# GELU through tanh, attention normalisation through a DMA transpose, and a scale folded into the last residual

## The chip, the core and the metric

The kernel runs on one core of a Trainium2 chip. The time is device microseconds for one execution, the median of several runs. The engines are TensorE (PE in the profile; PEld is its weight load), VectorE (DVE), ScalarE (ACT), GpSimd (POOL) and SyncE (SP), which issues most of the DMAs. Each engine works through its own list of instructions in order, and they meet through semaphores.

## The reference

One transformer block on 2048 tokens of width 640, in bf16: attention with 32 query heads of 20 columns over one shared key and value head, then a gated MLP of width 1536.

```python
x = A_x
h = x + _A_ref(_layernorm(x), A_wq, A_wk, A_wv, A_wo)
h2 = h + _B_ref(_layernorm(h), B_w_gate, B_w_up, B_w_down)

# _A_ref
q = (x @ wq) split into 32 heads; k = x @ wk; v = x @ wv
p = softmax(q k^T * 20 ** -0.5)
return (p v, heads side by side) @ wo

# _B_ref
g = x @ w_gate
u = x @ w_up
h = gelu(g, approximate=True) * u      # the tanh form
return h @ w_down
```

## The kernel before

The 16 token tiles of 128 rows are put into chunks: seven of two tiles, two of one (CHUNKS). A chunk's heads are cut into units, 32 in all; a unit is 512 query columns in four row groups. For each unit there are 16 packs, one for each tile of keys. A pack is four score matmuls (line 1083) that fill four PSUM banks of 512 columns, so that there are 512 packs and 2048 score tiles in all.

A score tile is made into exp in one of two ways. ScalarE takes one or two banks in one instruction (line 1423, tile pa). Or VectorE takes one bank (line 1509, tile pd): it computes an integer whose bits, read as bf16, are a rough exponential. Two shifted copies of that integer are added to it for accuracy, by POOL for both at once (line 1486), by POOL for one (line 1472), or by VectorE (line 1466). The product with the values (line 1162) runs over pa and over the three parts of pd. It collects a unit's sums and its row sums in one PSUM bank. Banks 0 to 5 are for scores; banks 6 and 7 are shared by those sums and by all other matmul jobs.

When a unit is done, its sums are copied to SBUF (osb, line 1189; two slots), transposed by four matmuls with the identity into a PSUM bank (on_job), and there divided by the row sums: a reciprocal (line 674, rcp) and one or two products (line 668) that write onq. When a chunk's units are all done, a DMA transposes onq into onT (line 699), the output projection follows and its result is added to xh (line 728). The second normalisation writes xn_tmp (line 472), and another DMA transpose on SP (line 464) makes xn2T.

The MLP of a chunk (a batch) runs while the next chunks' attention is under way. Its 12 gate blocks are worked in jobs of 512 columns, six for a batch of two tiles, three for a batch of one. A gate job's PSUM bank is copied to gbuf by VectorE (line 809). After the last gate job of the batch, ScalarE runs the GELU over gbuf in place, 1536 columns at a time (line 829), with a load of the function table in front and another one in front of the next exp. Each up job then multiplies gbuf by its bank (line 846), the down job adds its result to xh (line 864), and an output DMA stores it (line 862). For gate jobs that finish after the last exp, ScalarE takes the GELU straight from PSUM (line 811).

The order of every engine's list is made when the kernel is built, by a planner that plays the engines forward with a price for each instruction: c_act, c_dve, POOL_ADD and POOL_ADD2, in ns. Waiting work stands as jobs (matmul pieces for a bank) and tasks (one instruction), each with a priority; a task is placed when the plan says that its inputs are there. For each pack, issue_qk decides how many of its four tiles VectorE gets:

```python
burst = A > 3000.0                     # work queued on ScalarE, with the GELUs and their loads
...
elif burst:
    n = 4 if Dv < 2500.0 else 2
elif Dv > TH0:                         # work queued on VectorE; TH0 is 1500
    n = 0
elif Dv < TH2 or (SP2 and Dv < SP2D and len(pend[1]) + len(pend[2]) < 2 * SP2P
                  and stall(t, 1, fb) + 1382.0 - stall(t, 2, fb) - 956.0 > SP2G):
    n = 2
else:
    n = 1
```

Here pend holds shifted copies that nobody has made yet. VectorE makes them itself only when PADD_LEN of them wait. The functions that the change touches, and what calls them:

Of the kernel before, what the change touches and what calls it, by code (L numbers as in the profile page):

```python
# [3 lines left out]
ACT = mybir.ActivationFunctionType  # L4
# [190 lines left out]
def bass_sequential_preLN__grouped_kv_mqa__glu_gated_geglu__prompt_kernel(  # L195
# [36 lines left out]
    PE_TO = (15,)  # L232
    NA = 16
# [3 lines left out]
    NON = 8  # L237

# [10 lines left out]
    xn2T = sb("xn2T", [P, NC_D, 1024], BF16)  # L249
# [13 lines left out]
    osb = sb("osb", [P, 2, 512], BF16)  # L263
    rcp = sb("rcp", [P, 2, 16], F32)
    onq = sb("onq", [P, NON, D], BF16)
    onT = sb("onT", [P, 4, NC_D, P], BF16)
    gbuf = sb("gbuf", [P, NFC, 512], BF16)
    ident = sb("ident", [P, P], BF16)
# [32 lines left out]
    def c_mm(n):  # L301
        return n
# [12 lines left out]
    POOL_ADD = 635.0  # L315
    POOL_ADD2 = 1200.0
# [3 lines left out]
    SP2G = 300.0  # L320
# [4 lines left out]
    PADD_LEN = 2  # L325
# [7 lines left out]
    NP0 = 4  # L333
    WQA = 1
# [44 lines left out]
    slots = {"xt": list(range(NXT)), "q": list(range(NQ)), "onT": list(range(4)), "osb": [0, 1], "rcp": [0, 1]}  # L379
# [26 lines left out]
    def ln_group(ln, tiles, prio, done):  # L406
# [27 lines left out]
        def norm(t):  # L434
# [9 lines left out]
            def then(op):  # L444
# [12 lines left out]
                def free():  # L457
                    return ln == 0 or batch_of[t] < 2 or up_left[batch_of[t] - 2] == 0
# [35 lines left out]
    for b, tl in enumerate(BATCHES):  # L494
        for i, t in enumerate(tl):
            xcol[t] = (b % 2) * 512 + i * P
# [129 lines left out]
    def on_job(u, so):  # L626
        tl, gs = u["tiles"], u["groups"]
        nt, G = len(tl), len(gs)
        pieces = []
        for j in range(4):  # L630
            pieces.append((mm((lambda j: lambda b: ps[:, b * 512 + j * P:b * 512 + (j + 1) * P])(j),
                              osb[:, so, j * P:(j + 1) * P], ident[:], True, True), c_mm(128),
                           [("osb", so), "ident"]))

        def then(b):
            slots["osb"].append(so)
            sr = slots["rcp"].pop(0)
            v5 = bank(b).rearrange("p (j r e) -> p j r e", j=4, r=4)

            def c1(op):  # L640
                cnt = [0]
                parts = []
                rv = rcp[:, sr, :].rearrange("p (j r) -> p j r", j=4)
                if nt == 4:
                    g = gs[0]
                    o = onq[:, onslot[tl[0]]:onslot[tl[0]] + 4, 4 * Dh * g:4 * Dh * (g + 1)].rearrange(
                        "p j (r d) -> p j r d", r=4)
                    parts.append((o, slice(0, 4)))
                elif nt == 2:
                    for gi, g in enumerate(gs):  # L650
                        o = onq[:, onslot[tl[0]]:onslot[tl[0]] + 2, 4 * Dh * g:4 * Dh * (g + 1)].rearrange(
                            "p j (r d) -> p j r d", r=4)
                        parts.append((o, slice(2 * gi, 2 * gi + 2)))
                else:
                    o = onq[:, onslot[tl[0]], 4 * Dh * gs[0]:4 * Dh * (gs[-1] + 1)].rearrange(
                        "p (j r d) -> p j r d", j=4, r=4)
                    parts.append((o, slice(0, 4)))

                def c2(op):
                    cnt[0] += 1  # L660
                    if cnt[0] == len(parts):
                        free_bank(b)
                        slots["rcp"].append(sr)
                        unit_normed(u)

                for o, js in parts:
                    nj = js.stop - js.start
                    dve((lambda o, js, nj: lambda e: e.tensor_tensor(  # L668
                        o, v5[:, js, :, 0:Dh], rv[:, js, :].unsqueeze(3).to_broadcast([P, nj, 4, Dh]), ALU.mult))(
                            o, js, nj), c_dve(80 * nj), [("b", b), ("rcp", sr)],  # L670
                        [("onq", onslot[t], g) for t in tl for g in (gs if nj == 4 else [gs[js.start // 2]])],
                        0.9, c2)

            dve(lambda e: e.reciprocal(rcp[:, sr, :].rearrange("p (j r) -> p j r", j=4), v5[:, :, :, Dh]), 200,
                [("b", b)], [("rcp", sr)], 0.8, c1)

        def gate():
            return bool(slots["rcp"]) and all(x in on_sent for t in tl for x in on_before[t])
        jobs.append(_Job(("on", u["id"]), 1.5, pieces, then, gate))
# [56 lines left out]
    gate_left = [NFC] * len(BATCHES)  # L736
    up_left = [NFC] * len(BATCHES)
    copied = [[] for _ in BATCHES]
# [48 lines left out]

    def gate_job(b, fc):
        n = len(BATCHES[b]) * P
        k = per_job(b)  # L790
        ks = [x for i in range(k) for x in gkeys(b, fc + i)]

        def then(bk):
            def fin(op):
                free_bank(bk)
                gate_left[b] -= k
                copied[b].append(fc)
                if gate_left[b] == 0:
                    gelu(b)

            def fin2(op):
                free_bank(bk)
                gate_left[b] -= k
                up_job(b, fc)
                if gate_left[b] == 0 and copied[b]:
                    gelu(b)
            o, i = gview(b, fc, k), bview(bk, b, k)
            if state["exps_left"] > 0:
                dve(lambda e: e.tensor_copy(o, i), c_dve(n * k), [("b", bk)], ks, 1.0, fin)
            else:  # L810
                task(("act",), lambda e: e.activation(o, i, ACT.Gelu_apprx_tanh), ("gelu", c_act(n * k)), L_ACT,
                     [("b", bk)], ks, 1.0, fin2)
        jobs.append(_Job(("gate", b, fc), 5.0, gu_pieces(wg_sb, b, fc), then, lambda: g_free(b)))

    def gelu(b):
        k = per_job(b)
        fcs = sorted(copied[b])
        runs = []
        n = len(BATCHES[b]) * P
        most = max(k, 1536 // n)  # L820
        for fc in fcs:
            if runs and runs[-1][1] == fc and fc + k - runs[-1][0] <= most:
                runs[-1][1] = fc + k
            else:
                runs.append([fc, fc + k])
        for f0, f1 in runs:
            v = gview(b, f0, f1 - f0)
            ks = [x for fc in range(f0, f1) for x in gkeys(b, fc)]
            task(("act",), (lambda v: lambda e: e.activation(v, v, ACT.Gelu_apprx_tanh))(v),
                 ("gelu", c_act(n * (f1 - f0))), L_ACT, ks, ks, 1.0,  # L830
                 (lambda f0, f1: lambda op: [up_job(b, fc) for fc in range(f0, f1, k)])(f0, f1))

    def up_job(b, fc):
        n = len(BATCHES[b]) * P
        k = per_job(b)
        ks = [x for i in range(k) for x in gkeys(b, fc + i)]

        def then(bk):
            def fin(op):
                free_bank(bk)  # L840
# [4 lines left out]
            o, i = gview(b, fc, k), bview(bk, b, k)  # L845
            dve(lambda e: e.tensor_tensor(o, i, o, ALU.mult), c_dve(n * k), [("b", bk)] + ks, ks, 1.0, fin)  # L846
# [875 lines left out]
```

The softmax here doesn't subtract the row's maximum and nothing guards it: scores larger than these inputs give would overflow.

## Time and profile before

| | |
|---|---|
| median of 9 runs | 805.67 us (803.52 to 806.87) |
| the profiled execution | 803.7 us, its span 801.8 us |
| mean granted TensorE clock | 0.979 |
| ACT busy | 749.8 us (94%) |
| PE busy | 689.9 us (86%) |
| DVE busy | 627.3 us (78%) |
| POOL busy | 585.4 us (73%) |
| score tiles | 1461 on ScalarE, 587 on VectorE |

The span is the time from the first to the last instruction; the rest of the execution's time lies around it. In the groups of the profile each row has a line of the kernel, an engine, an operation, what it writes and reads, its shape and count, then its busy time, the mean duration of one instruction and the idle time of the engine just before. An instruction's duration can overlap its neighbour's on the same engine, so that count times mean is more than the busy time.

### The profile page before, as it was taken

What the parts mean: (1) busy time and instruction counts of PE and PEld (TensorE: products, weight loads), DVE (VectorE), ACT (ScalarE), POOL (GpSimd) and SP (SyncE); (2) the same over time, 40 slices, a digit from 0 to 9 for tenths busy, and PEclk for the clock granted to TensorE, in tenths of its full rate; (3) what the DMA queues carried; (4) which work ended last, traced back from release to release, by engine and by line L of the source; (5) the groups of instructions that cost most, each with busy time, mean ns of one, the idle gap of its engine ahead of it and who ended that gap; (6) DMA issues with size and microseconds to landing.
All of it is one profiled execution on the core that took longest, in us unless ns stands there. A gap on an engine that the chain in (4) does not pass through costs nothing.

```text
span 801.8 us, 29858 instructions
## 1 busy us (share of the span) xinstructions
PE 689.9 (86%) x13162; PEld 331.5 (41%) x13162; DVE 627.3 (78%) x1156; ACT 749.8 (94%) x1065; POOL 585.4 (73%) x624
## 2 busy tenths in 40 slices
PE   4687778979978998789988799888998899887998
PEld 3332223534434443344434344334444444343457
DVE  7968889777888678977788777988779767878864
ACT  5899999999989999899999999999999999999981
POOL 4587878868767677766878678877787768776760
PEclk9999999999999899999999999999999999999999
DMA  6680001000100000000000000000010000100000
GB/s 193 128 308 2 2 10 26 3 2 2 36 18 3 2 19 19 18 3 3 19 18 19 2 3 19 19 19 2 3 35 19 4 2 19 19 18 11 11 19 18
DMA packets 40288, 21.96 MB, mean 27 GB/s; under 512 B 31328, under 2 KB 38880, under 8 KB 40160
## 3 DMA queue, kind: packets, MB, share of 16 engines
q1 hardware_dynamic: 38848, 19.61, 9.5%
q8 instruction: 105, 1.72, 0.9%
q10 hardware_dynamic: 1312, 0.44, 0.2%
q14 instruction: 23, 0.19, 0.1%
HBM read 10.21 MB, written 2.62 MB: 16 GB/s over the span
## 4 chain that ended last, share of the span: by engine, by line
PE 47%; DVE 25%; ACT 24%; issue 2%; DMA 1%; POOL 1%; POOLq 0%; DVEq 0%
ACT pa L1423 24%; PE ps L510 18%; DVE pd L1509 15%; PE ps L1083 14%; PE ps L1162 13%; PE ps L506 3%; DVE pd L1466 3%; DVE xn_tmp L472 2%; DVE osb L1189 1%; DVE stats L403 1%; DVE qT L580 1%; DVE xh L728 1%; DMA onT<-onq 1%; DVE onq L668 0%; DVE ln_vb L415 0%
## 5 line engine op out<-in xcount | busy, mean ns | idle before, releaser
L1423 ACT ACTIVATE pa<-ps 128x512 bf16<-128x512 f32 (+1 forms) x1012 | 698.6, 849 | 24.1 <-PE ps L1083 19.2
L1486 POOL TENSOR_TENSOR pd<-pd,shifts 128x512 int32<-128x512 int32 x517 | 534.1, 1041 | 168.4 <-DVE pd L1509 159.7
L1509 DVE TENSOR_SCALAR pd<-ps 128x512 uint16<-128x512 f32 x587 | 395.4, 688 | 139.9 <-PE ps L1083 129.2
L1162 PE MATMUL ps<-pd,v_ext 128*32 128x512 bf16 x1761 | 273.6, 395 | 28.1 <-DVE osb L1189 21.5
L1162 PE MATMUL ps<-pa,v_ext 128*32 128x512 bf16 x1461 | 263.6, 391 | 2.7 <-ACT pa L1423 1.3
L1083 PE MATMUL ps<-qT,kT 32*128 32x512 bf16 x2048 | 205.3, 388 | 66.9 <-DVE pd L1509 41.1
L1083 PEld LDWEIGHTS ps<-qT,kT 32*128 32x128 bf16 x2048 | 58.8, 91 | 233.2 <-DVE pd L1509 163.7
L1162 PEld LDWEIGHTS ps<-pd,v_ext 128*32 128x32 bf16 x1761 | 74.5, 97 | 78.5 <-issue 33.8
L1162 PEld LDWEIGHTS ps<-pa,v_ext 128*32 128x32 bf16 x1461 | 70.3, 96 | 42.5 <-issue 29.4
L510 PE MATMUL ps<-xn2T,wg_sb 128*32 128x256 bf16 (+1 forms) x1720 | 65.2, 276 | 0.1
L510 PE MATMUL ps<-xn2T,wu_sb 128*32 128x256 bf16 x1680 | 65.2, 277 | 0.1
L510 PE MATMUL ps<-wd_sb,gbuf 128*32 128x320 bf16 x1344 | 64.3, 301 | 0.2 <-DVE onq L668 0.2
L510 PE MATMUL ps<-xn1T,wq_pad 128*32 128x256 bf16 (+1 forms) x1440 | 51.2, 267 | 0.2
L510 PEld LDWEIGHTS ps<-xn2T,wu_sb 128*32 128x32 bf16 x1680 | 43.0, 98 | 18.5 <-issue 10.1
L510 PEld LDWEIGHTS ps<-xn2T,wg_sb 128*32 128x32 bf16 x1720 | 41.7, 97 | 17.3 <-issue 11.4
L510 PEld LDWEIGHTS ps<-wd_sb,gbuf 128*32 128x32 bf16 x1344 | 33.5, 96 | 23.7 <-issue 11.8
L510 PEld LDWEIGHTS ps<-xn1T,wq_pad 128*32 128x32 bf16 x1440 | 33.9, 98 | 13.7 <-issue 8.6
L846 DVE TENSOR_TENSOR gbuf<-ps,gbuf 128x512 bf16<-128x512 f32 x48 | 32.9, 686 | 6.6 <-PE ps L506 6.4
L1466 DVE TENSOR_SCALAR pd<-pd 128x512 uint16<-128x512 uint16 (+2 forms) x66 | 37.8, 594 | 0.0
L1472 POOL TENSOR_TENSOR pd<-pd,shifts 128x256 int32<-128x256 int32 x48 | 30.2, 635 | 3.5 <-DVE pd L1509 3.0
L403 DVE BATCH_NORM_STATS2 stats<-xh 128x6 f32<-128x320 bf16 x64 | 29.9, 477 | 1.2 <-DMA xh<-in_A_x_dram 1.0
L510 PE MATMUL ps<-wo_sb,onT 128*32 128x320 bf16 x600 | 28.5, 301 | 0.9 <-DMA onT<-onq 0.6
(71 smaller groups left out, 357.6 us busy)
## 6 DMA issues: line engine op xcount, KB each, us to landing
out_dram<-xh SPq DMA_DIRECT2D x16, 160.0 KB, 1.8
xh<-in_A_x_dram SPq DMA_DIRECT2D x3, 640.0 KB, 6.8
wg_sb<-in_B_w_gate_dram SPq DMA_DIRECT2D x1, 1920.0 KB, 9.1
wu_sb<-in_B_w_up_dram SPq DMA_DIRECT2D x1, 1920.0 KB, 13.4
wd_sb<-in_B_w_down_dram SPq DMA_DIRECT2D x1, 1920.0 KB, 18.0
wo_sb<-in_A_wo_dram SPq DMA_DIRECT2D x1, 800.0 KB, 5.1
gbuf<-in_A_wq_dram ACTq DMA_DIRECT2D x1, 400.0 KB, 4.8
gbuf<-in_A_wq_dram SPq DMA_DIRECT2D x1, 400.0 KB, 7.4
```

The costliest lines, as they stand in the source:

```text
L403: dve(lambda e: e.bn_stats(stats[:, ln, t, 6 * h:6 * h + 6], xh[:, t, h * HALF:(h + 1) * HALF]), 395, [key], [("st", ln, t, h)], prio, c)
L472: tk.fn = lambda e: e.tensor_scalar(xn_tmp[:, s, :], xh[:, t, :], mv[:, ln, t, 0:1], ln_r[:, ln, t:t + 1], ALU.subtract, ALU.mult)
L506: return e.matmul(o(b), l, r, start=st, stop=sp)
L510: ins = e.matmul(o(b)[a, :], l[:, a], r, start=st, stop=sp, tile_position=(0, 32 * j))
L846: dve(lambda e: e.tensor_tensor(o, i, o, ALU.mult), c_dve(n * k), [("b", bk)] + ks, ks, 1.0, fin)
L1083: ins = e.matmul(bank(b), kT4[32 * r:32 * r + 32, kt * P:(kt + 1) * P], qT[32 * r:32 * r + 32, s, :], start=True, stop=True, tile_position ...
L1162: ins = e.matmul(ps[32 * r:32 * r + 32, ab * 512:(ab + 1) * 512], v_ext[:, it["kt"], it["w"], :], it["ap"], start=st, stop=(j in ends), ti ...
L1423: op = plan.commit("act", lambda e: e.activation(dst, src, ACT.Exp, scale=SM_SCALE), cost, L_ACT, [("b", b0 + i) for i in range(n)], [("pa ...
L1466: return e.tensor_scalar(pd[:, w, a], pd[:, 0, a], float(CH_SHIFT[w]), None, ALU.add)
L1472: return e.tensor_tensor(pd32[:, w, h], pd32[:, 0, h], shifts[:, w - 1:w].to_broadcast([P, 256 * k]), ALU.add)
L1486: return e.tensor_tensor(pd32[:, 1:3, h], pd32[:, 0, h].unsqueeze(1).to_broadcast([P, 2, 256]), shifts[:].unsqueeze(2).to_broadcast([P, 2, ...
L1509: op = plan.commit("dve", lambda e: e.tensor_scalar(pd[:, 0, s * 512:(s + 1) * 512], bank(b), CH_A, CH_B, ALU.mult, ALU.add), c_dve(512), ...
```

## The change

- **GELU.** While exps are left, the gate bank is scaled by the square root of 0.044715 on its way into gbuf. VectorE squares it into a new tile zt (six slots) and makes the cubic (z + 1) times o in one instruction. ScalarE takes tanh of that, 512 columns at a time. The up job's bank is multiplied by (tanh + 1), and the product goes once more by gbuf. The up job starts when its tanh is done, not when the batch's GELU is. Gate jobs after the last exp keep the GELU instruction.
- **Normalisation.** For units 0 to 29 a DMA transpose on SP brings osb into a new tile onr (two slots); the reciprocal and one product read it there. Units 30 and 31 keep the identity matmuls.
- **Residual.** The factor 2 times that square root stays in gbuf and is taken out where the down-projection is added to xh.
- **Sizes and prices.** xn2T has three parts of 256 columns in place of two of 512. POOL's prices, SP2G and PADD_LEN are other numbers, and ScalarE's queue counts waiting tanh tasks without a table load.

```diff
+    PE_ON = (30, 31)
+    NZ = 6
...
-    xn2T = sb("xn2T", [P, NC_D, 1024], BF16)
+    xn2T = sb("xn2T", [P, NC_D, 768], BF16)
...
+    onr = sb("onr", [P, 2, 512], BF16)
+    zt = sb("zt", [P, NZ, 512], BF16)
...
+    def c_dve2(n):
+        return n / 1.92 + 150.0
-    POOL_ADD = 635.0
-    POOL_ADD2 = 1200.0
+    POOL_ADD = 580.0
+    POOL_ADD2 = 1010.0
-    SP2G = 300.0
+    SP2G = 200.0
-    PADD_LEN = 2
+    PADD_LEN = 3
...
+    def normed(u, so, v, key, done):
...
+            tk.fn = lambda e: e.reciprocal(rcp[:, sr, :].rearrange("p (j r) -> p j r", j=4), v4[:, :, :, Dh])
...
+            dve(lambda e: e.tensor_tensor(o, i0, i1, ALU.mult), 400, [key, ("rcp", sr)],
+                [("onq", onslot[t], g) for t in tl for g in gs], 0.9, c2)
...
+    def on_job(u, so):
+        if u["id"] in PE_ON:
...
+        tk = _Task(("sp",), None, 1330, 1500, [("osb", so)], [], 0.5, None, lambda: bool(slots["onr"]))
...
+            tk.fn = lambda e: e.dma_start_transpose(onr[:, s, :].rearrange("p (j i) -> p j i", j=4), osb[:, so, :])
...
     def gate_job(b, fc):
...
+                sq = (lambda e: e.tensor_tensor(z, o, o, ALU.mult))
...
+                    dve(sq, c_dve2(w), ks, [("z", s)], 1.0, c2)
+            def c2(op):
+                dve(lambda e: e.scalar_tensor_tensor(z, z, 1.0, o, ALU.add, ALU.mult), c_dve(w), [("z", s)] + ks,
+                    [("z", s)], 1.0, c3)
+            def c3(op):
+                task(("act",), lambda e: e.activation(zt[:, s, 0:w], zt[:, s, 0:w], ACT.Tanh, scale=GC / GK),
+                     c_act(w) + 45.0, L_ACT, [("z", s)], [("z", s)], 1.0, lambda op: up_job(b, fc, s))
             if state["exps_left"] > 0:
-                dve(lambda e: e.tensor_copy(o, i), c_dve(n * k), [("b", bk)], ks, 1.0, fin)
+                dve(lambda e: e.tensor_scalar(o, i, GK, None, ALU.mult), c_dve(w), [("b", bk)], ks, 1.0, c1)
...
-    def gelu(b):
...
-            dve(lambda e: e.tensor_tensor(o, i, o, ALU.mult), c_dve(n * k), [("b", bk)] + ks, ks, 1.0, fin)
+            if s is None:
+                dve(lambda e: e.scalar_tensor_tensor(o, i, 2.0 * GK, o, ALU.mult, ALU.mult), c_dve(w),
+                    [("b", bk)] + ks, ks, 1.0, fin)
+                return
...
+                dve(lambda e: e.tensor_tensor(o, z, o, ALU.mult), c_dve2(w), [("z", s)] + ks, ks, 1.0, fin)
+            dve(lambda e: e.scalar_tensor_tensor(z, z, 1.0, i, ALU.add, ALU.mult), c_dve(w),
+                [("b", bk), ("z", s)], [("z", s)], 1.0, c1)
...
-            dve(lambda e: e.tensor_tensor(xh[:, t, h * HALF:(h + 1) * HALF], xh[:, t, h * HALF:(h + 1) * HALF],
-                                          bank(bk, HALF), ALU.add), c_dve(HALF),
+            x = xh[:, t, h * HALF:(h + 1) * HALF]
+            dve(lambda e: e.scalar_tensor_tensor(x, bank(bk, HALF), 0.5 / GK, x, ALU.mult, ALU.add), c_dve(HALF),
...
+    def act_tasks():
+        return sum(tk.cost for tk in tasks if tk.engs[0] == "act" and not isinstance(tk.cost, tuple))
...
-        if state["tab"] == "gelu" or any(tk.engs[0] == "act" for tk in tasks):
-            A += sum(tk.cost[1] for tk in tasks if tk.engs[0] == "act" and isinstance(tk.cost, tuple)) + 1300.0
+        A += act_tasks()
-        burst = A > 3000.0
+        burst = A > BURST
```

BURST is 3000.

## Prediction

> **What bounds the kernel now.** I read the page's busy times first, then the groups with their forms kept apart, then the windows of the long middle, and last the timeline around one GELU. Busy times and groups:
>
> ```profile
> PE 689.9 (86%) x13162; PEld 331.5 (41%) x13162; DVE 627.3 (78%) x1156; ACT 749.8 (94%) x1065; POOL 585.4 (73%) x624
> ...
> L1423 ACT ACTIVATE pa<-ps 128x1024 bf16<-128x1024 f32 x449 | 487.3, 1088 | 2.5 <-PE ps L1083 2.5
> L1509 DVE TENSOR_SCALAR pd<-ps 128x512 uint16<-128x512 f32 x587 | 395.4, 688 | 139.9 <-PE ps L1083 129.2
> L1423 ACT ACTIVATE pa<-ps 128x512 bf16<-128x512 f32 x563 | 357.7, 659 | 21.6 <-PE ps L1083 16.7 <-PE ps L1162 0.2
> ...
> L846 DVE TENSOR_TENSOR gbuf<-ps,gbuf 128x512 bf16<-128x512 f32 x48 | 32.9, 686 | 6.6 <-PE ps L506 6.4
> ...
> L809 DVE CAST gbuf<-ps 128x512 bf16<-128x512 f32 x42 | 28.7, 684 | 0.3 <-PE ps L510 0.2
> ...
> L1466 DVE TENSOR_SCALAR pd<-pd 128x512 uint16<-128x512 uint16 x43 | 21.3, 500 | 0.0
> ...
> L829 ACT ACTIVATE gbuf<-gbuf 128x1536 bf16<-128x1536 bf16 x14 | 20.0, 1475 | 0.1
> L668 DVE TENSOR_TENSOR onq<-ps,rcp 128x160 bf16<-128x160 f32 x56 | 16.1, 318 | 0.7
> ...
> L829 ACT ACT_TABLE_LOAD x7 | 9.0, 1283 | 0.1
> L1423 ACT ACT_TABLE_LOAD x7 | 9.0, 1283 | 0.0
> ```
>
> The 2048 softmax tiles of 512 columns are shared: ScalarE takes 2 x 449 + 563 = 1461, VectorE (DVE) 587. A tile costs ScalarE 0.478 us (the page's 698.6 us for both forms, by 1461) and DVE 0.673 (395.4 by 587). DVE's idle time (139.9) is waiting for the next scores; ScalarE has almost none. The windows say it for the middle:
>
> ```profile
> core 0: us, PE busy (x) PEld busy (x) DVE busy (x) ACT busy (x) POOL busy (x), PEclk, DMA share, GB/s
> 40.00:760.00 720.00, 627.77 (x12058) 291.33 (x12050) 573.10 (x1006) 700.54 (x994) 550.54 (x560) 0.98 0.08 21
> 120.00:160.00 40.00, 35.59 (x700) 16.94 (x698) 34.94 (x64) 39.65 (x58) 32.76 (x34) 1.00 0.07 15
> 400.00:440.00 40.00, 33.61 (x632) 14.76 (x624) 35.18 (x66) 38.54 (x58) 31.27 (x32) 1.00 0.09 19
> ```
>
> In these 720 us ScalarE is busy 97.3% and DVE 79.6%. So ScalarE's work sets the length, and each tile that DVE takes off it shortens the whole. The chain of waits gives PE 47%, DVE 25%, ACT 24%: the three hand one set of score banks round, so no bank is late for long. Around one GELU:
>
> ```profile
> 447.74 3.68 DVE L1509 TENSOR_SCALAR pd<-ps 128x512 uint16<-128x512 f32 x6
> 448.08 1.28 ACT L829 ACT_TABLE_LOAD   x1
> 449.38 2.86 ACT L829 ACTIVATE gbuf<-gbuf 128x1536 bf16<-128x1536 bf16 x2
> 452.24 1.28 ACT L1423 ACT_TABLE_LOAD   x1
> ```
>
> ScalarE leaves the exps for 5.4 us, and DVE does six tiles in a row meanwhile: the planner's burst rule buys back part of the stop.
>
> **ScalarE, step by step.** Out: seven such stops, 20.0 + 9.0 + 9.0 = 38.0 us. In: 42 tanh of 512 columns (as many as L809 has gates; the six GELUs after the last exp stay). A third of the 1475 ns GELU is 0.49 us, the 512-wide exp lasts 0.66, its share per tile is 0.478. Bounds 20.0 and 27.7 us; I take 0.52, or 21.8, since the input is SBUF as in the GELU. Saved: 16.2 us (10 to 18). This assumes no table load between exp and tanh. The trace of before has no tanh. The Trainium skill, "ScalarE: Activation LUTs" (the section on table sets), lists tanh beside exp in one set; no run here shows it.
>
> **DVE.** The scaled copy takes the place of L809's cast, and the (tanh+1) times up that of L846's product: both read one PSUM bank, nothing changes. New, 42 times each: the square and the last product (two bf16 inputs in SBUF) and the cubic, of the scalar-tensor-tensor kind. No row shows any of them. The nearest for the first two is L1466, SBUF to SBUF with 16-bit data, 277 to 690 ns for 512 columns with a mean of 500. For the cubic it is L846, two tensors, 686; the least is 445, which a 640-wide L472 took while POOL was idle. Sum 42 x (0.50 + 0.68 + 0.50) = 70.6 us, bounds 42 and 87. Here a rule speaks against the change. L1466's spread shows what DVE meets beside POOL's adds: 277 at best, 690 at worst, with POOL busy 73%. The skill's "GPSIMD Engine Reference" (Specifications) says that GpSimd shares its SBUF interfaces with DVE and contends with instructions that have two SBUF inputs, which all three are. By that rule all 126 stand at the slow end, 87 us, and the sum below comes out 7 us worse; I stay with the mean row, which already has that POOL beside it.
>
> Off DVE: 28 of the units do one wide product in place of two of 0.287 us; the 320-wide row lasts 0.492, so 2 us at least, 8 if SBUF data go at 0.28; I take 4. The adds on L1466 (37.8 us in all) wait for three in a row instead of two, and the planner now prices POOL at 1010 against 1041 measured: between none and all go to POOL. I take half, 19 us. POOL gets 23 more pairs of 1.04 us on 585; its 168 us of idle time before L1486 covers that. Net on DVE: 70.6 - 4 - 19 = +47.6 us.
>
> **Normalisation by DMA.** 30 units lose their PE job, 15.6 of the 16.1 us of identity matmuls, and a PSUM bank for that time. PE is not what ends last, so I credit nothing; the most that it could bring is the 3.3 us for which PE waited on L668. SP gets 30 more transposes, each 1.2 us to issue; the like (onT) land after 2.6. By PE, the crossing at 453.6 to 455.9 us took 2.3. So a unit is some 1.5 us later. That is hidden: a unit comes every 23 us and osb has two slots. Queued behind SP's new wait are the xn2T and onT transposes and the output stores, which sit idle for most of 23 us; without this cover, 30 x 1.5 = 45 us. The skill's "VectorE: DVE Perf Modes" (The three transpose paths) speaks against it too, with 1309 ns by DMA for a 128x128 block and 390 by TensorE: four blocks and 30 units would be 110 us if they lay on the path. The trace has no waiter on that path, so I count zero. The down-projection's scaling is one instruction for one, also zero, as is xn2T in three parts.
>
> **A new wait.** The old GELU found casts that were long done. Each tanh waits for a cubic just finished, and ScalarE's next exps queue behind it, then the banks, then PE. Bounds: 0, and 42 x 0.69 = 29 us, a whole DVE instruction each time. I take a tenth, 3 us, since the planner puts the tanh only where its cubic is due and ScalarE usually runs behind.
>
> **The sum.** Let the middle grow by t, and x tiles go from DVE to ScalarE, ScalarE keeping its 97.3% and DVE reaching a share u:
> 0.973 (720 + t) = 700.5 - 16.2 + 0.478 x, and u (720 + t) = 573.1 + 47.6 - 0.673 x.
> With u = 0.796 as now: t = +11, x = 57. With u = 0.862: t = -10, x = 13. With 0.88: t = -16, x = 1. What is u? The five busiest windows of 40 us (two are shown) have DVE at 33.9 to 35.2, mean 0.862, and ScalarE at 0.974 in them: a DVE that busy does not starve ScalarE. The others are low for want of work or of a permitted second tile; the change brings the work, and it lowers the gain asked of a second tile (SP2G 300 to 200). I take 0.862. With the new wait (3 us through the same equations, +2) t is -8.2. The profiled execution took 803.7 us, 1.9 around its span of 801.8, and so 795.5; it lies 2.0 below the median of 805.67. Forecast 797.5.
>
> **Rivals.**
> 1. *DVE goes no further.* The planner gives a pack no DVE tile when DVE's queue passes 1500 ns, and the burst rule's extra tiles go with the stops. It decides from 16.2 / 0.478 = 34 tiles, that is, DVE under 553 tiles. Price +11, or 817; +20 if no add leaves DVE. For it: DVE's light windows (28 of 40 us) stayed light. Against: the five busy ones. Chance 0.27.
> 2. *The tanh wait in full.* 29 us through the equations is +18, less 10: +8, or 814. For it: DVE's real 686 against 600 in the plan. Against: ScalarE is late as well. 0.08.
> 3. *More than forecast.* All adds to POOL and u at 0.88: -24, or 781. 0.08.
> 4. *The change does not rid ScalarE of loads*, tanh needing its own: up to 84 x 1.283 = 108 us less the 18 of now, 90 more on ScalarE: +57 in place of -10, 863. 0.02.
> 5. *They cancel*, within 1.6 us. 0.05.
>
> The forecast case has 0.50. Faster 0.50 + 0.08 = 0.58, same 0.05, slower 0.37; "same" is 0.2%, 1.6 us, about what a measurement of this kernel can tell. The range goes from 785, short of most of rival 3, to 819, past rival 1's first price; the rest left out is its upper price, rival 4 and some of 2, 2 in 10 in all. The forecast case's own range is 788 to 803.
>
> **What would show it.** Right: one ACT table load after the first instead of 15, 42 tanh of 0.5 to 0.6 us, DVE near 86% in the middle, L1509's successor at 565 to 590 tiles, and ScalarE still at 97%. Wrong: fewer than 553 DVE tiles (rival 1); ScalarE idle in front of tanh by over 10 us (rival 2); the three new DVE forms near 690 each; PE waiting on the unit's DMA.

## The result: slower by 0.7%, and the profile after

The changed kernel takes 811.37 us (median of 16 runs, 807.48 to 814.35) against 805.9 of the kernel before, over 53 runs: ratio 1.0071, interval 1.0061 to 1.0082. The forecast was 797.5, faster; the sign is wrong. The profiled execution took 810.74 us, its span 808.9, the clock 0.983. First the busy times (the page) and the groups with their forms kept apart (busy us, mean ns, idle before):

```profile
PE 687.2 (85%) x12639; PEld 320.5 (40%) x12639; DVE 657.3 (81%) x1169; ACT 746.2 (92%) x1093; POOL 621.7 (77%) x620
...
L1472 ACT ACTIVATE pa<-ps 128x1024 bf16<-128x1024 f32 x461 | 501.2, 1090 | 2.8 <-PE ps L1130 2.4 <-PE ps L1209 0.4
L1558 DVE TENSOR_SCALAR pd<-ps 128x512 uint16<-128x512 f32 x561 | 380.2, 687 | 113.3 <-PE ps L1130 104.7
L1472 ACT ACTIVATE pa<-ps 128x512 bf16<-128x512 f32 x565 | 359.2, 654 | 28.3 <-PE ps L1130 22.6 <-PE ps L1209 2.0
...
L845 DVE SCALAR_TENSOR_TENSOR zt<-zt,gbuf 128x512 bf16<-128x512 bf16 x43 | 30.6, 712 | 0.0
L849 ACT ACTIVATE zt<-zt 128x512 bf16<-128x512 bf16 x43 | 29.6, 689 | 0.9 <-DVE zt L845 0.7
...
L838 DVE TENSOR_TENSOR zt<-gbuf 128x512 bf16<-128x512 bf16 x43 | 28.0, 652 | 0.5
L664 DVE TENSOR_TENSOR onq<-onr,rcp 128x320 bf16<-128x320 bf16 x30 | 24.8, 826 | 0.4
L889 DVE TENSOR_TENSOR gbuf<-zt,gbuf 128x512 bf16<-128x512 bf16 x43 | 24.4, 568 | 0.3
...
L650 DVE RECIPROCAL rcp<-onr 128x16 f32<-128x16 bf16 x30 | 7.4, 246 | 5.3 <-DMA onr<-osb 5.3
...
L378 ACT ACT_TABLE_LOAD x1 | 1.3, 1283 | 1.8 <-issue 1.8
L854 ACT ACT_TABLE_LOAD x1 | 1.3, 1283 | 0.0
```

ScalarE makes 2 x 461 + 565 = 1487 tiles, 26 more than before, and VectorE 561. Only two table loads are left. ScalarE's busy time falls by 3.6 us only, and its idle time, the span less the busy time, grows from 52.0 to 62.7. The three new VectorE rows stand at 24 to 31 us each, the product of the normalisation (L664) at 826 ns, and in front of the reciprocal (L650) VectorE waits 5.3 us for the DMA. In the kernel before it waits 7.9 us at that place (L674), 6.4 of them for TensorE's transposes, but not in the first unit. The middle, and ten microseconds near its start, in the windows; the last line is the same ten in the kernel before:

```profile
core 0: us, PE busy (x) PEld busy (x) DVE busy (x) ACT busy (x) POOL busy (x), PEclk, DMA share, GB/s
60.00:70.00 10.00, 7.09 (x74) 1.75 (x74) 6.88 (x12) 6.80 (x12) 7.47 (x8) 0.83 0.01 2
40.00:760.00 720.00, 620.04 (x11442) 277.34 (x11437) 596.59 (x1007) 692.81 (x1015) 584.51 (x555) 0.98 0.12 26
60.00:70.00 10.00, 7.65 (x126) 2.97 (x125) 8.52 (x14) 9.68 (x16) 7.95 (x9) 1.00 0.01 2
```

In the middle VectorE is busy 82.9% (596.59 of 720) and ScalarE 96.2%; the forecast had 86.2 and 97.3. The first line is unlike the middle: ScalarE is busy 6.80 of 10 us, at a granted clock of 0.83, against 9.68 and 1.00 before. The timeline shows what comes before it, the first unit's normalisation (start, length, engine, what it waited for):

```profile
54.34 1.20 SPq L692 DMA_TRANSPOSE onr<-osb  x1
...
60.42 0.25 DVE L650 RECIPROCAL rcp<-onr 128x16 f32<-128x16 bf16 x1 [2.68 <-DMA onr<-osb]
...
61.95 0.61 PE L1130 MATMUL ps<-qT,kT 32*128 32x512 bf16 x4 [3.39 <-DVE pd L1558]
...
62.61 1.15 ACT L1472 ACTIVATE pa<-ps 128x512 bf16<-128x512 f32 x2 [2.44 <-PE ps L1130]
```

The transpose goes out at 54.34 and lands 6.05 us later. VectorE stands in front of it for 2.68 us, its next evictions queue behind, the score matmuls wait 3.39 us for a bank that VectorE should free, and ScalarE waits 2.44 us for those scores.

### The profile page after: what moved, and what is told of

Same layout as the page of the kernel before. It is cut to its first block, busy times and chain, and to the rows that moved or that the text cites. A ratio compares the mean times of both kernels' runs of the same rounds, so it can differ in the third digit from the quotient of the medians.

```text
span 808.9 us, 28882 instructions
## 1 busy us (share of the span) xinstructions
PE 687.2 (85%) x12639; PEld 320.5 (40%) x12639; DVE 657.3 (81%) x1169; ACT 746.2 (92%) x1093; POOL 621.7 (77%) x620
## 4 chain that ended last, share of the span: by engine, by line
PE 38%; ACT 27%; DVE 23%; POOL 6%; DMA 4%; issue 2%; POOLq 0%
ACT pa L1472 26%; PE ps L519 13%; DVE pd L1558 12%; PE ps L1130 11%; PE ps L1209 10%; POOL pd L1535 5%; PE ps L515 3%; DMA onr<-osb 3%; DVE onq L664 2%; DVE zt L838 1%; ACT zt L849 1%; DVE osb L1236 1%; DVE stats L412 1%; DVE zt L845 1%; DVE xn_tmp L481 1%
## 5 line engine op out<-in xcount | busy, mean ns | idle before, releaser
L1472 ACT ACTIVATE pa<-ps 128x512 bf16<-128x512 f32 (+1 forms) x1026 | 718.2, 850 | 31.1 <-PE ps L1130 24.9
L1535 POOL TENSOR_TENSOR pd<-pd,shifts 128x512 int32<-128x512 int32 x555 | 594.7, 1088 | 140.4 <-DVE pd L1558 135.7
L1558 DVE TENSOR_SCALAR pd<-ps 128x512 uint16<-128x512 f32 x561 | 380.2, 687 | 113.3 <-PE ps L1130 104.7
L1209 PE MATMUL ps<-pd,v_ext 128*32 128x512 bf16 x1683 | 264.7, 389 | 20.2 <-DVE osb L1236 11.0
L1209 PE MATMUL ps<-pa,v_ext 128*32 128x512 bf16 x1487 | 264.0, 389 | 11.1 <-POOL pd L1535 8.9
L519 PE MATMUL ps<-xn2T,wu_sb 128*32 128x256 bf16 x1680 | 62.0, 275 | 3.4 <-DVE gbuf L852 3.1
L519 PE MATMUL ps<-wd_sb,gbuf 128*32 128x320 bf16 x1252 | 59.7, 301 | 0.0
L519 PEld LDWEIGHTS ps<-xn2T,wu_sb 128*32 128x32 bf16 x1680 | 40.5, 96 | 23.7 <-issue 14.4
L412 DVE BATCH_NORM_STATS2 stats<-xh 128x6 f32<-128x320 bf16 x64 | 29.9, 477 | 1.2 <-DMA xh<-in_A_x_dram 1.1
L890 DVE SCALAR_TENSOR_TENSOR zt<-zt,ps 128x512 bf16<-128x512 bf16 x43 | 29.0, 675 | 2.0 <-PE ps L519 1.0
L845 DVE SCALAR_TENSOR_TENSOR zt<-zt,gbuf 128x512 bf16<-128x512 bf16 x43 | 30.6, 712 | 0.0
L849 ACT ACTIVATE zt<-zt 128x512 bf16<-128x512 bf16 x43 | 29.6, 689 | 0.9 <-DVE zt L845 0.7
## 6 DMA issues: line engine op xcount, KB each, us to landing
wd_sb<-in_B_w_down_dram SPq DMA_DIRECT2D x1, 1920.0 KB, 18.6
```

The source lines that it names most:

```text
L412: dve(lambda e: e.bn_stats(stats[:, ln, t, 6 * h:6 * h + 6], xh[:, t, h * HALF:(h + 1) * HALF]), 395, [key], [("st", ln, t, h)], prio, c)
L519: ins = e.matmul(o(b)[a, :], l[:, a], r, start=st, stop=sp, tile_position=(0, 32 * j))
L845: dve(lambda e: e.scalar_tensor_tensor(z, z, 1.0, o, ALU.add, ALU.mult), c_dve(w), [("z", s)] + ks, [("z", s)], 1.0, c3)
L849: task(("act",), lambda e: e.activation(zt[:, s, 0:w], zt[:, s, 0:w], ACT.Tanh, scale=GC / GK), c_act(w) + 45.0, L_ACT, [("z", s)], [("z", ...
L890: dve(lambda e: e.scalar_tensor_tensor(z, z, 1.0, i, ALU.add, ALU.mult), c_dve(w), [("b", bk), ("z", s)], [("z", s)], 1.0, c1)
L1209: ins = e.matmul(ps[32 * r:32 * r + 32, ab * 512:(ab + 1) * 512], v_ext[:, it["kt"], it["w"], :], it["ap"], start=st, stop=(j in ends), ti ...
```

## The experiments

All times are medians; each ratio is to the kernel before, run beside it, with its 95% interval. The planner writes the order anew for every edit, so that an edit also reshuffles the plan; "shaken" below means the same kernel with a switch price of 107 in place of 105, which changes nothing else.

**Which part is it?** The first kernel undoes the prices, the second the DMA normalisation, the third both; the fourth gives the kernel before the new prices. In e2 and e3 the change's one wide product stays, now read from PSUM.

```diff
e1, e3:  POOL_ADD 580 -> 635, POOL_ADD2 1010 -> 1200, SP2G 200 -> 300, PADD_LEN 3 -> 2
e2, e3:  PE_ON = (30, 31)  ->  tuple(range(32))
e4 (the kernel before):  POOL_ADD 635 -> 580, POOL_ADD2 1200 -> 1010, SP2G 300 -> 200, PADD_LEN 2 -> 3
```

> The changed kernel with the four prices of the kernel before (POOL_ADD 635, POOL_ADD2 1200, SP2G 300, PADD_LEN 2). Theory P (POOL is starved: with the new prices it makes nearly all shifted copies, 555 pairs of 1.09 us, and PE waits 44 us for it where it waited 7): about 36 us of copies go back to VectorE, PE's waits for POOL fall under 15 us, and the time falls by 3 to 6 us, to 805 to 808. Theory V (VectorE's time is what is short, the three new instructions of a gate and the slower product): the copies on VectorE cost it more score tiles, under 550, and the time stays or rises, 811 to 816. Theory N (the DMA normalisation is what costs): no change beyond 1.6 us.

> The changed kernel with all 32 units normalised through TensorE (PE_ON is every unit), the GELU and the prices as changed. Theory N: the wait for the transposed sums and the 826 ns product go; 4 to 7 us faster, 804 to 807. Theory V: VectorE gains about 30 x 0.25 us, 7 us of its time, which the equations of the prediction turn into 3 us: 808. Theory P: no change beyond 1.6 us.

> The tanh GELU and the folded scale alone: normalisation through TensorE for all units, and the four old prices. Theory V: with copies and GELU both on VectorE, 808 to 815, no better than the kernel before, and VectorE at most 83% busy in the middle. Theory P: at or under the kernel before, 800 to 806. Theory N: as P.

> The kernel before with the four new prices and nothing else. Theory P: slower than before by 3 to 6 us, 809 to 812, with PE waiting over 25 us for POOL. Theory V: faster, since VectorE is relieved of up to 36 us of copies: 797 to 804, with over 600 score tiles on VectorE. Theory N: no statement.

| kernel | us | ratio, interval | last exp at, us | left after it |
|---|---|---|---|---|
| before | 805.9 | | 775.0 | 26.8 |
| after | 811.4 | 1.0071 (1.0061 to 1.0082) | 779.9 | 29.0 |
| e1, old prices | 812.1 | 1.0084 (1.0069 to 1.0100) | 779.7 | 32.0 |
| e2, TensorE normalisation | 805.4 | 0.9992 (0.9981 to 1.0004) | 772.7 | 32.1 |
| e3, both (tanh GELU alone) | 803.5 | 0.9976 (0.9964 to 0.9988) | 773.1 | 29.7 |
| e4, before with new prices | 801.2 | 0.9948 (0.9933 to 0.9964) | 767.8 | 29.9 |

The last two columns are of the profiled executions, which lie up to 2.2 us off the medians. The DMA normalisation costs 6.0 us with the new prices (811.4 less 805.4) and 8.7 with the old. The prices are not the harm; they gain 4.5 us on the kernel before. The tanh form alone gains about 2 us (e3), a fraction of what was forecast, and with the new prices nothing (e2). So theory N holds. P had e4 slower than before, and V had e3 no better than before and over 600 tiles on VectorE in e4 (it has 590): both are out.

**Is it the transfers, the first unit, or VectorE's time?** e5 takes the first unit alone back to TensorE; e6 is e2 with 30 transposes of osb that nobody reads; e7 is e2 with a useless copy of 160 columns from PSUM in units 0 to 29, planned as 9.5 us of VectorE in all and measured as 7.9.

```diff
e5:  PE_ON = (30, 31)  ->  (0, 30, 31)
e6:  + e.dma_start_transpose(onr[...], osb[:, so, :])     # units 0 to 29, beside the matmuls
e7:  + dve(lambda e: e.tensor_copy(scr[:], v[:, 0:160]), ...)   # ahead of the product, units 0 to 29
```

> The changed kernel with unit 0 normalised through TensorE as well; units 1 to 29 stay with the DMA. In the changed kernel unit 0's transpose was issued at 54 us, while the weights load, and landed after 6.1 us in place of 2.4; VectorE stood 2.7 us in front of the reciprocal, and ScalarE was busy 6.8 of the 10 us from 60 on. Theory L (that one crossing behind the weight loads is the cost of the DMA way): about 3 us faster, 807 to 809, and ScalarE busy over 9.5 us from 60 to 70. Theory S (the product that reads SBUF, 826 ns against 485, on all 30 units): no more than 0.5 us faster. Theory W (VectorE waits for many transposes): under 1 us faster.

> Normalisation through TensorE for all units as in the run with all units there (805.4), and beside it 30 DMA transposes of the same tile that nobody reads: SP and the DMA engines have their work, the consumers do not wait. Theory D (the transfers themselves disturb: SP's queue, SBUF, the other transposes): 808 to 812. Theories L, S and W: 804.5 to 806.5.

> As the run with all units through TensorE (805.4), and a copy of 160 columns from PSUM, about 0.32 us, that nobody needs, between the reciprocal and the product of units 0 to 29: 9.5 us more of VectorE in all, as much as the product from SBUF cost more. Theory S, and the equations of the prediction (VectorE's microseconds count 0.43): 4 us slower, 809 to 810. Theories L and W: under 1.5 us slower.

e5 took 808.1 us (1.0028, 1.0010 to 1.0046): with one unit of 30 back on TensorE, 3.3 us of the 6.0 are gone, and ScalarE's busy time in 60 to 70 us goes from 6.80 to 9.97. e6 took 806.3 (1.0005, 0.9994 to 1.0015): the transfers as such cost about 1 us, and theory D (808 to 812) is out. e7 came out at 802.7 (0.9958, 0.9941 to 0.9976), 2.7 us faster than e2, where every theory had it level or slower: its plan gave VectorE 550 tiles in place of 568, and VectorE is less busy in the middle than in e2 (587 us against 598). So e7 says nothing on the slow product, and a plan's luck is worth some 3 us.

**How large is the plan's luck?** The DMA normalisation (with its wide product) was put into the kernel before alone, and four kernels were shaken.

```diff
e8:   the kernel before, with normed() and on_job() of the change, PE_ON = (30, 31)
e9, e10, e11, e12:  before, e8, e3, after, each with  SW = 105.0  ->  107.0
```

> The kernel before with the DMA normalisation and its one wide product alone; GELU and prices as before. Theories L, S and D: the same price as beside the new GELU, 6 to 9 us slower than before, 811 to 815. A theory that the two new burdens on VectorE only hurt together: within 3 us of before.

> The kernel before with the planner's price of a mode switch at 107 ns in place of 105: no work is added or taken, but the lists of all engines come out in another order. It says how far a plan's luck alone moves the time. Theory J (luck is worth some 3 us either way, which is why 9.5 us more of VectorE came out 2.7 us faster): between 801 and 810, off 805.7 by 1 us or more. Theory K (luck is worth under 1 us and the run with the idle copy needs a cause of its own): 805 to 806.5.

> The same 2 ns on the kernel before with the DMA normalisation alone (811.4). Theory J: 806 to 816, and still over its partner without the DMA way. Theory K: 810.5 to 812.5.

> The same 2 ns on the run with the tanh GELU alone (803.5). Theory J: 799 to 808. Theory K: 802.5 to 804.5.

> The same 2 ns on the changed kernel (811.4). Theory J: 806 to 816. Theory K: 810.5 to 812.5. Over the four pairs, the size of the differences is the luck of a plan, against which every difference of these runs has to be read.

e8 took 811.4 (1.0070, 1.0043 to 1.0097), 5.5 us more than before; but shaken (e10) only 804.4 (0.9990, 0.9973 to 1.0007). That is below its partner without the DMA (e9), where theory J had it still above: beside the old GELU the DMA normalisation costs 5.5 us in one plan and nothing in the other. The other three pairs lie close: before 805.9 and 806.7, e3 803.5 and 802.3, after 811.4 and 812.0. So luck is mostly about 1 us and can be 7, and single kernels with another order settle nothing under some 3 us. With the tanh GELU the three plans with the DMA (after, e12 and e1) took 811.4, 812.0 and 812.1, and three with TensorE (e2, e3 and e11) 805.4, 803.5 and 802.3; there the price is larger than the luck. What held in all five kernels whose first transpose goes out behind the weight loads is the hole: ScalarE busy 6.7 to 8.2 of the 10 us from 60 on, against 9.3 to 10.0 in the other kernels.

Beside all these differences runs the granted clock. Runs of the kernel before at 0.970 took 806.6 us in the mean, those at 0.977 took 804.6; and the kernels differ in it, 0.968 to 0.987 for the changed one, 0.987 to 1.000 for e3, 0.985 to 0.994 for e17 below. Whether a plan with fewer waits gets its clock, or the clock is a cause of its own, was not tried.

**The hole, with the order unchanged.** In the timeline SP issues the gate, up and down weights at 40.1 to 41.3 us, three times 1920 KB; the last lands 18.6 us after its issue, at 59.9, and the transpose issued at 54.34 lands half a microsecond after that, at 60.4. e14 moves these three issues and nothing else: the lists of TensorE, VectorE, ScalarE and GpSimd are the same, instruction for instruction. The luck of the plan has no part in it.

```diff
-    for nm, o, v in (("wo", ...), ("wg", ...), ("wu", ...), ("wd", ...)):          # plan.free["sp"] > 30000
+    for nm, o, v, at in (("wo", ..., 0), ("wg", ..., 64e3), ("wu", ..., 82e3), ("wd", ..., 104e3)):
+    # ... and plan.ops["pe"][-1].end > at
```

> The changed kernel with nothing moved but three DMA issues: the loads of the gate, up and down weights go out on SP at about 64, 82 and 104 us, between the transposes of the first units, in place of 40-43 us; every instruction of TensorE, VectorE, ScalarE and GpSimd keeps its place. Their first use is after 145 us. L (the first unit's transpose stands behind the weight loads): it lands in 2.4-2.7 us in place of 6.1, ScalarE's busy time in 60-70 us goes from 6.8 to 9 or more, the granted clock there does not fall to 0.83, and the time falls by 3 us (2.5 to 4.5) to 808.4. If the loads are not the cause: landing still 5-6 us, time 811.4. Since the order of the work is the same, the plan's luck has no part in the difference.

The loads went out at 55.9, 74.8 and 94.8 us, each right behind one of the first three transposes. It took 808.35 us (1.0042, 1.0027 to 1.0056): 3.0 less by the medians, 2.3 by the ratios, and the profiled span is 2.4 shorter. At the same granted clock (0.981 to 0.985) the two kernels still lie 2.1 us apart in the mean, 810.6 and 808.5, so the hole's price does not rest on the clock of the whole run. The same instructions in its timeline, its window from 60 us, and the time from issue to landing of all 30 transposes, here and in the changed kernel:

```profile
54.68 1.20 SPq L692 DMA_TRANSPOSE onr<-osb  x1
...
57.99 0.25 DVE L650 RECIPROCAL rcp<-onr 128x16 f32<-128x16 bf16 x1
```

```profile
60.00:70.00 10.00, 8.34 (x133) 2.99 (x129) 7.07 (x11) 9.68 (x16) 9.93 (x11) 1.00 0.29 117
```

```profile
DMA to landing us min/median/max: 2.4/2.4/4.1
```

```profile
DMA to landing us min/median/max: 2.4/2.4/6.1
```

The reciprocal starts 2.4 us earlier and waits for nothing; ScalarE is busy 9.68 us in the window and the clock is whole. The first transpose lands in 2.4 us; the longest landing, 4.1 us, is now a later one.

**The rest of the DMA's price.** e13 is e5 with the transposes planned to land 3.0 us after their issue in place of 1.5, so that the planner sets the reciprocal later in VectorE's list; e17 is the changed kernel with e14's and e13's edits together.

```diff
-        tk = _Task(("sp",), None, 1330, 1500, [("osb", so)], ...
+        tk = _Task(("sp",), None, 1330, 3000, [("osb", so)], ...
```

> The first unit and the last two through TensorE as in e5 (808.1 us), and the other 29 transposes planned to land 3.0 us after their issue in place of 1.5, so that the planner puts the reciprocal later in VectorE's order. W (what is left of the price of the DMA path is VectorE standing before a transpose that has not landed, with evictions queued behind it): no wait of the reciprocal on a DMA is left, and the time falls by most of the 2.7 us between e5 and e2, to 805-806. S (the product from SBUF at 0.83 us in place of 0.49, and POOL's additions stretched beside it): no change, 807.5-808.5. J (the plan's luck): anything within 3 us of 808, the waits not deciding.

> The changed kernel with e14's later weight loads and e13's later planned landing of the transposes (3.0 us) together; 30 units still go by DMA and their products still read SBUF. If the two causes are the whole price of the DMA path (811.4 against 805.4 with TensorE, e2): 804.5 to 806.5, no wait of the reciprocal on a DMA, ScalarE 9.3 or more in 60-70 us. If the slow product and the stretched additions of POOL have a part (S): 807 to 809. J: the plan moves by up to 3 us either way, so a result of 806.5 to 807 tells nothing.

e13 took 805.2 us (0.9990, 0.9972 to 1.0008), 2.9 less than e5; e17 805.86 (1.0002, 0.9991 to 1.0014), against 805.4 for e2 with TensorE. Groups and windows of e17:

```profile
L664 DVE TENSOR_TENSOR onq<-onr,rcp 128x320 bf16<-128x320 bf16 x30 | 26.0, 868 | 0.3
...
L650 DVE RECIPROCAL rcp<-onr 128x16 f32<-128x16 bf16 x30 | 7.3, 243 | 0.0
```

```profile
60.00:70.00 10.00, 7.34 (x115) 2.73 (x115) 8.24 (x13) 9.47 (x17) 10.00 (x11) 1.00 0.38 151
40.00:760.00 720.00, 624.35 (x11592) 281.16 (x11592) 600.12 (x1018) 698.30 (x1025) 586.61 (x558) 1.00 0.11 26
```

No wait on a transpose is left, and the product is as slow as before, 868 ns. So the two mendings take back 5.5 of the 6.0 us with the slow product still there, which leaves it no large part. The share of the weights, 2.3 to 3.0 us, is settled by e14. That the other 2.5 are VectorE's waits (3.5 us are left in e14) agrees in two kernels, each with a new plan and a higher granted clock, so it is argued and not shown. The sum of such waits is no price by itself: in the kernel before it is 7.9 us, and e4, among the fastest, has 10.1.

**What is VectorE's time worth in the middle?** e16 is e3 without the square and the cubic: tanh is taken of the scaled gate. e15 shakes e4. e18 is e4 with the one wide product, from PSUM.

```diff
e16:  def c1(op): free_bank(bk); - square - cubic;  tanh reads o in place of zt
e15:  e4 with SW = 105.0 -> 107.0
e18:  e4 with normed() of the change, PE_ON = tuple(range(32))
```

> The tanh GELU alone (e3, 803.5 us) with the square and the cubic left out: tanh is taken of the scaled gate itself, so 86 VectorE instructions go (28.0 + 30.6 us in the changed kernel) and part of the GELU isn't computed. V (the prediction's equations: an added microsecond of VectorE costs 0.43 us of the middle, since it passes tiles to ScalarE): some 58 us less of VectorE give 25 us, 778-780. Other theory, P (POOL and the plan's order bound the tiles that VectorE can turn, not its time): a gain of under 10 us, 794 or more, with VectorE's tiles near 570-585 and its busy share in the middle under 0.79.

> The old kernel with the four new prices (e4, 801.2 us) and the same shaking of the plan as in e9 (switch cost 107 in place of 105). J (e4's gain of 4.5 us is the plan's luck): 804-806, no better than the old kernel. Other theory, K (longer additions for POOL are worth it, since a pair of two costs 1.17 us of POOL against 0.64 for one): 801-802 again.

> The old kernel with the new prices (e4, 801.2 us; shaken e15, 800.3) and the one part of the change that VectorE may gain by: the normalisation's product as one wide instruction from PSUM (32 of 0.485 us in place of 60, 15.5 us against 18.1), transposes by TensorE as before. By the equations 2.6 us of VectorE are 1.1 us; by e16 (56 us of VectorE gave 11 us) 0.5 us. So 800 to 801, and no difference that can be told from e4.

e16 took 792.4 us (0.9838, 0.9820 to 0.9857), 11.1 less than e3 for 56 us less of VectorE: neither the 25 that the equations gave, nor the under 10 of theory P. The middle of e3 and of e16:

```profile
40.00:760.00 720.00, 625.83 (x12002) 286.98 (x12002) 609.68 (x1064) 698.58 (x1027) 568.35 (x553) 0.99 0.08 21
```

```profile
40.00:760.00 720.00, 638.64 (x12298) 295.82 (x12294) 579.98 (x1011) 702.28 (x1039) 564.42 (x572) 1.00 0.08 21
```

VectorE's busy time in these 720 us falls by 30, its share from 0.847 to 0.806, and its tiles rise by 11 only (561 to 572): much of the freed time went to nothing. The 11 tiles are 5.3 us of ScalarE's time; the rest of the 11.1 is less waiting, 2.5 us of it behind the last exp. A microsecond of VectorE is worth 0.20 us here, in one plan, not 0.43. POOL's additions get shorter too (1086 ns to 1049 in the mean), and e16 can't tell the two apart. e15 took 800.3 (0.9935, 0.9915 to 0.9954): the new prices are worth about 5 us to the kernel before in two plans of two, and this is the fastest complete kernel of the study, ahead of both kernels. (A pair takes POOL 1041 ns in the mean there and 1173 at most in the kernel before, so the 1.17 us of its expectation is not the usual price.) e18 took 804.2 (0.9977, 0.9963 to 0.9991), 3 to 4 us more than e4 and e15 and than the 800 to 801 expected, for 2.6 us less of VectorE: another reshuffled plan, so the gain of the prices is 1.7 to 5.6 us.

## Why the prediction was wrong, step by step

**The step that failed first** is "The trace has no waiter on that path, so I count zero". The term at nothing cost 6 us (e2; 8.7 with the old prices), enough to turn the sign: without it the change is level with the kernel before. And the trace of before had a waiter on that path. VectorE waits 7.9 us in front of its reciprocal, and the very crossing that the text timed, 453.6 to 455.9 us, ends in one of these waits:

```profile
L674 DVE RECIPROCAL rcp<-ps 128x16 f32<-128x16 f32 x32 | 8.0, 250 | 7.9 <-PE ps L510 6.4 <-PE ps L506 1.3
...
455.88 0.26 DVE L674 RECIPROCAL rcp<-ps 128x16 f32<-128x16 f32 x1 [1.69 <-PE ps L510]
```

The cover that the text named, two osb slots and 23 us between units, was real but covered something else. It keeps units from waiting for slots. It does not cover the waiting instruction's own engine: the reciprocal holds its place in VectorE's list, and what is queued behind it are evictions that TensorE and ScalarE need within a microsecond. The text listed the DMAs that SP would hold up, and not this. The bound of 45 us "without this cover" did contain the price. And the transposes' time was read as a median (2.6 us of onT), while the first one goes out with the weight loads still in flight. "PE waiting on the unit's DMA" was named as a sign; it was VectorE that waited, 5.3 us. This step is not the whole miss: of the 13.9 us between forecast and result, 7.9 are left in e2, and those lie in the tail and the share u, below.

The page "VectorE: DVE Perf Modes" of the Trainium skill (The three transpose paths) had spoken against the step with 1309 ns by DMA and 390 by TensorE a block. Here four blocks by one DMA landed in 2.4 us at the median; with the plan told to expect 3.0 us, the dearer path cost nothing that the runs can tell (805.9 against 805.4).

**The middle and the tail.** The forecast's span was 801.8 - 8.2 = 793.6. The profiled span is 808.9, so 15.3 more: 6.4 more ScalarE work (746.2 against 739.8, for 26 added tiles instead of 13) and 8.9 more idle time. By place, 13.1 lie ahead of the last exp and 2.2 after it. Without the DMA's part (e2: span 804.8, in an execution 1.2 us above its median) 11.2 remain: 5.9 ahead of the last exp, and 5.3 behind it, where the text had put nothing. In the twelve kernels with the whole tanh form 28.3 to 32.1 us follow the last exp, mean 30.1; in seven without it 25.9 to 30.5, mean 27.6. The down-projection shows it: its matmuls in the full-width form, which are those that run after the scores, are 48 before, 71 after, and 95 in e2 (0.30 us each; the first of them starts at 785.3, 781.8 and 774.5 us). Why more of the MLP is left over was not tried.

**ScalarE's term was right.** Out 38.0 us; with 26 more tiles at 0.478 (12.4) and 3.6 us less in all, the 43 tanh take 38.0 - 12.4 - 3.6 = 22.0 us, where 42 were put at 21.8. (By its own row it is 29.6 us; the neighbours overlap it.) No table load lies between exp and tanh: rival 4 is out, and the Trainium skill's "ScalarE: Activation LUTs" (the section on table sets), which lists the two in one set, agrees with the two loads in all. The mean of its row, 689 ns with the overlap of its neighbours, is above the 500 to 600 that were named as a sign, and misled nothing else. In front of the tanh ScalarE waits 0.7 us for the cubics, not 3: rival 2 is out.

**VectorE's terms** were each off, and cancel. The three new operations cost 28.0 + 30.6 + 24.4 = 83.0 us, not 70.6; the wide product is 25.8 us against 18.1, 7.7 more instead of 4 less; the additions left VectorE almost wholly, 37.8 to 1.6, 36 us instead of 19. By rows that is a net of 54.5 against 47.6. By VectorE's busy time, which counts overlapping instructions once, it is 657.3 - 627.3 + 26 x 0.673 = 47.5: the forecast's sum, by luck. The rows that were to stand near 690 if the forecast was wrong stand at 652, 712 and 568; the first two are nearer to that than to the 500 and 680 it took, the third is nearer to its 500. Here the rule that the text set aside was nearer than the mean row: the page "GPSIMD Engine Reference" (Specifications) on GpSimd and VectorE contending for SBUF, put at 87 us there. But not all instructions stand at the slow end: the medians are 460, 681 and 416 ns. The product shows it apart, by its source (the lines give minimum, median and maximum ns):

```profile
L664 DVE TENSOR_TENSOR onq<-onr,rcp x30: 475/777/1324, 60.7 to 740.5; 128x320 bf16<-128x320 bf16 x30
L664 DVE TENSOR_TENSOR onq<-ps,rcp x2: 480/486/492, 761.9 to 784.2; 128x320 bf16<-128x320 f32 x2
```

```profile
L664 DVE TENSOR_TENSOR onq<-ps,rcp x32: 475/481/493, 55.4 to 776.9; 128x320 bf16<-128x320 f32 x32
```

From PSUM it never takes more than 493 ns; from SBUF, the same columns take 475 to 1324. But e17, as slow in this product and level with e2, speaks against it as what decided.

**The share u.** "A DVE that busy does not starve ScalarE ... the change brings the work" chose 0.862; it came to 0.829 (0.830 in e2, 0.834 in e17). In the prediction's own equations 0.829 gives t = +0.4 in place of -10, an estimate that leaves the middle as long as before. Measured in e2, without the DMA's part, the last exp comes 2.3 us earlier than before, where the forecast had 8.2. The low share is rival 1's side: the tiles fell to 561, under the 565 that was named as a sign but not to its 553, and the time stands between the forecast and its 817. The flaw is the premise under both, that VectorE's share is a given and its time turns into tiles. e16 freed 56 us and got 11 tiles, where the equations with u held would have moved some 50. The planner's rule for a pack (its queue, the stall that it works out, the additions still pending) hands out tiles, and free time alone changed little in e16. Which of these conditions held it back was not tried. By e16's price 83 us of new VectorE work cost about 16.6 us, an estimate, as much as the 16 that ScalarE saved.

**What stays open:** why the prices gain 5 us without the tanh form (e4, e15) and lose 2 with it (e2 805.4, e3 803.5), what of the last 2.5 us of the DMA's price is VectorE's waits, what the granted clock does by itself, what holds u down, and the longer tail.

## What to carry to other kernels

When a step goes from an engine to a DMA, don't ask only whether its consumer has slack: ask which in-order engine will stand in front of the landing and what is queued behind it there, take the worst landing in the trace (bulk loads in flight) and not the median, and give the planner a landing time that holds. Before an engine's freed time is priced in work taken over, look for the rule that hands the work out; here 56 us free became 11 tiles. In a kernel whose order is planned, compare edits that leave the order alone, or shake the plan: a price moved by 2 ns changed one kernel by 7 us.

## What the runs showed of the hardware

- Beside GpSimd's additions, some VectorE instructions that read two SBUF operands take about three times as long as others of their kind: the product of 320 columns 475 to 1324 ns, the square of 512 360 to 1262. Most of the cubics do not (673 ns at least, 681 the median, 1368 at most). GpSimd's own addition is stretched too: after the change, the 159 that overlap a square, a cubic or one of the two products from SBUF by over 0.1 us take 1.21 us in the mean, the other 402 take 1.03. Its longest is 1485 ns after the change, and 1173 before it, with the median the same:

```profile
L1535 POOL TENSOR_TENSOR pd<-pd,shifts x555: 1030/1037/1485, 32.7 to 780.2; 128x512 int32<-128x512 int32 x185
```

```profile
L1486 POOL TENSOR_TENSOR pd<-pd,shifts x517: 1031/1037/1173, 32.5 to 775.2; 128x512 int32<-128x512 int32 x173
```

- The first transpose, issued while weights stream in, lands in 6.1 us (4.7 to 5.8 in e1, e8, e10 and e12) in place of 2.4, and ScalarE is busy 6.80 us in the ten from 60 on, against 9.68 with the loads moved (e14).
- After the wait of 3.39 us that TensorE had there, the granted clock of that stretch is 0.83 (0.54 in e12, whose plan has the same hole); with the wait gone (e14) it is 1.00.
